# A second MLP whose two layers both run as seven-product block schemes, in alternate phases

## The chip, the cores and the metric

One core of a Trainium2 chip runs the whole program in one launch. The metric is device time in microseconds; the kernel before takes 1431.7 us (median of 3 runs, 1430.7 to 1431.89).

## The reference, cut to what matters

An attention between `x` and a small `state` gives 4352 tokens of 512 values, which go through two MLPs with FF = 2048. The change lies in the second one:

```python
def _moe2_ref(x, w_in, w_out, alpha):        # x 4352 x 512
    h = x @ w_in                             # w_in 512 x 2048
    g = np.maximum(h, 0.0) + alpha * np.minimum(h, 0.0)
    return (g @ w_out).astype(np.float32)    # w_out 2048 x 512
```

## The kernel before, in words

Each matrix product keeps fp32 accuracy by splitting an operand into a high part (`hi_`, an ACT copy that rounds to fp32r) and a low part (`lo_`, a DVE subtraction of two SBUF tiles, raw minus high; in a few places on POOL). Three matmuls replace one: high by high, high by low, low by high.

The first MLP runs in `steps`: nine token tiles times 16 blocks of FF, with the attention, the decoding of weights and the preparation of the second MLP hung onto step numbers by `at(...)`. A tile's result goes to DRAM (`xd`) from `out_end`.

The second MLP is `second()`. Tokens are cut into five superblocks; superblock s has two halves of `HALF[s]` tokens (512, 512, 384, 384, 384). Layer one is a Strassen-Winograd scheme: the two halves of the tokens and the two halves of the contraction make 2 x 2 blocks, and each of the 8 pairs q of FF blocks needs seven products instead of eight. One product is one `h_item`: six matmuls with a weight block standing and `HALF[s]` tokens streaming. `h_after` adds products into the four results and applies the slope (`slope`: ReLU of -h on ACT, then one DVE operation with `beta_sb`). `w_sums` and `w_split` make the weight sums and their high and low parts, again for each of the 40 (s, q). Layer two is direct: `o_item` takes one FF block of one half, its activations standing in 128-token pieces and 512 columns of `w_out` streaming, three matmuls per piece, 16 FF blocks accumulating.

The order is written out by hand. `ev` holds layer one's products at places 0, 1, 2, ... and layer two's items at 36 + 1.75 m, sorted; so both layers alternate item by item, layer two some 36 products behind. Each engine works its own instructions in program order; SP (`ld`) issues nearly all DMAs, in program order too. Tiles come from pools: `U` 80 buffers of 128 x 512, `V` 10 of 128 x 1024, PSUM two pools of four banks (`pa` for accumulators, `pp`). An instruction that needs a buffer waits until its last reader is done.

The lines of the profile: L759 layer one's matmuls, L824 layer two's, L73 the high parts, L76 the low parts, L661 weight sums, L726 sums of x, L768 and L770 the slope, L784 adds from PSUM, L788 a copy from PSUM, L744 and L646 the loads of weights, L847 the stores of the output.

Of the kernel before, what the change touches and what calls it, by code (L numbers as in the profile page):

```python
# [34 lines left out]
ROWS = S + NS  # L35
TOK = NB * ROWS
HALF = [512, 512, 384, 384, 384]
# [3 lines left out]
def kernel_body(ctx: ExitStack, tc: tile.TileContext, x, state, w1i, w1o, w2i, w2o, alpha, out):  # L41
# [55 lines left out]
    wod = dp.tile([NF, 128, 1024], F32, name="wod")  # L97
# [544 lines left out]
    def wr_get(q):  # L642

        for kh in range(2):
            t = U(f"wr{q}{kh}")
            ld.dma_start(out=t, in_=wid[q % 8, kh])  # L646
            WR[q, kh] = t
# [4 lines left out]
    def w_sums(q):  # L652
        r0, r1 = [parts(WR[q, kh]) for kh in range(2)]
        a11, a21, a12, a22 = r0[:, :, 0], r0[:, :, 1], r1[:, :, 0], r1[:, :, 1]
        sa, sb = U(f"sa{q}"), U(f"sb{q}")
        WR[q, 2], WR[q, 3] = sa, sb
        va, vb = parts(sa), parts(sb)
        s2, s1, s3, s4 = va[:, :, 0], va[:, :, 1], vb[:, :, 0], vb[:, :, 1]
        for o, a, b, op in ((s1, a21, a22, ALU.add), (s2, s1, a11, ALU.subtract),
                            (s3, a11, a21, ALU.subtract), (s4, a12, s2, ALU.subtract)):  # L660
            dve.tensor_tensor(out=o, in0=a, in1=b, op=op)  # L661
            yield

    def w_split(q, n):

        t, h = WR.pop((q, n)), U(f"wh{q}{n}", F32R)
        if n == 0:
            t = parts(t)[:, :, 0]
            h, l = [h[:, v * 256:(v + 1) * 256].rearrange("p (k c) -> p k c", k=2) for v in range(2)]
        else:  # L670
            l = U(f"wl{q}{n}", F32R)
        hi_(h, t)
        yield
        yield
        lo_(l, t, h)
        if n == 0:
            WU[q, 0] = h, l
            return
        h, l = parts(h), parts(l)
        for e, k in enumerate({1: (1, 3), 2: (5, 4), 3: (6, 2)}[n]):  # L680
            WU[q, k] = (h[:, :, e], l[:, :, e])

    def pairs(j):
        return 2 * j, 2 * j + 1

    FO = list(range(NF))

    def w2o_put(n):

        raw = G.pop(("dec", ("w2o", FO[n])))  # L690
        h, l = U(f"woh{n}", F32R), U(f"wol{n}", F32R)
        hi_(h, raw)
        WR["o", n] = h, l
        yield
        lo_(l, raw, h)

    def w2o_store(n):
        for e, t in enumerate(WR.pop(("o", n))):
            ld.dma_start(out=wod[FO[n], :, e * 512:(e + 1) * 512], in_=t.bitcast(F32))


    NSUP = len(HALF)

    BASE = [2 * sum(HALF[:s]) for s in (0, 1, 2, 4, 3)]
    C0 = [BASE[s // 2] + (s % 2) * HALF[s // 2] for s in range(2 * NSUP)]
    HO = [0, 5, 4, 6, 1, 2, 3]
    XR, XB, XT, HB, GT, GR, GS, OA = {}, {}, {}, {}, {}, {}, {}, {}
# [4 lines left out]
    def xr_load(s, kh, tk):  # L712
        w = wof(s)
        v = V(f"xr{s}{kh}{tk}")[:, :2 * w].rearrange("p (k c) -> p k c", k=2)
        c0 = C0[2 * s + tk]
        ld.dma_start(out=v, in_=xd[2 * kh:2 * kh + 2, :, c0:c0 + w].rearrange("k p c -> p k c"))
        XR[s, kh, tk] = v

    def x_sums(s, m):

        for kk in range(2):
            b11, b21, b12, b22 = [XR[s, kh, tk][:, kk] for tk in range(2) for kh in range(2)]
            XT[s, m, kk] = U(f"xt{s}{m}{kk}")[:, :wof(s)]
            x, y = {3: lambda: (b22, b12), 2: lambda: (XT[s, 3, kk], b11), 1: lambda: (b12, b11),
                    4: lambda: (b21, XT[s, 2, kk])}[m]()
            dve.tensor_tensor(out=XT[s, m, kk], in0=x, in1=y, op=ALU.add if m == 2 else ALU.subtract)  # L726

    def x_prep(s, step):

        w = wof(s)  # L730
        n = HO[step]
        for kk in range(2):
            b11, b21, b12, b22 = [XR[s, kh, tk][:, kk] for tk in range(2) for kh in range(2)]
            src = {0: b11, 1: b21, 2: b22}.get(n)
            if src is None:
                src = XT[s, {3: 4, 4: 1, 5: 2, 6: 3}[n], kk]
            h, l = U(f"xh{s}{n}{kk}", F32R)[:, :w], U(f"xl{s}{n}{kk}", F32R)[:, :w]
            hi_(h, src)
            lo_(l, src, h, pool if kk else dve)
            XB[s, n, kk] = (h, l)  # L740

    def wo_get(m):
        t = V(f"wv{m}", F32R)
        ld.dma_start(out=t.bitcast(F32), in_=wod[FO[m % NF]])  # L744
        WB["o", m] = t

    def h_item(n):
        q, k = divmod(n, 7)
        s, p = q // 8, HO[k]
        bank = {0: "A", 1: "A", 5: "D", 6: "D", 3: "D", 4: "E", 2: "E"}[p]  # L750
        if p in (0, 5, 4):
            HB[q, bank] = PS(f"hB{q}{p}")
        ps = HB[q, bank][:, :wof(s)]
        wh, wl = WU.pop((q, p))
        m = 0
        for kk in range(2):
            xh, xl = XB[s, p, kk]
            for a, b in ((wh, xh), (wh, xl), (wl, xh)):
                pe.matmul(ps, a[:, kk], b, start=(p in (0, 5, 4) and m == 0), stop=(m == 5),  # L759
                          skip_group_check=True)  # L760
                m += 1

    def slope(q, e, tk, h, g=None):

# [7 lines left out]
    def h_after(n):

        q, k = divmod(n, 7)
        w = wof(q // 8)
        p = HO[k]
        A, D, E = [HB[q, b][:, :w] if (q, b) in HB else None for b in "ADE"]

        def tmp(name):
            GT[q, name] = U(f"{name}_{q}")[:, :w]  # L780
            return GT[q, name]

        def plus(out, a, b):
            dve.tensor_tensor(out=out, in0=a, in1=b, op=ALU.add)  # L784
            return out

        if p == 0:
            act.copy(tmp("p1"), A)  # L788
        elif p == 5:
            plus(tmp("u2"), D, GT[q, "p1"])  # L790
        elif p == 1:
            slope(q, 0, 0, A)
        elif p == 6:
            h = plus(tmp("u3"), D, GT[q, "p1"])
            plus(h, E, h)
            slope(q, 1, 1, h, h)
        elif p == 3:
# [6 lines left out]
    def o_split(m):
        t, f = m // NF, FO[m % NF]
        w = wof(t // 2)
        g = GR.pop((t, f))
        v = V(f"gs{m}", F32R)
        h, l = v[:, :w], v[:, 512:512 + w]
        hi_(h, g)  # L810
        lo_(l, g, h)
        GS[m] = (h, l)

    def o_item(m):
        t, r = divmod(m, NF)
        gh, gl = GS.pop(m)
        wt = WB.pop(("o", m))
        wh, wl = wt[:, :512], wt[:, 512:]
        for k in range(wof(t // 2) // 128):
            if r == 0:  # L820
                OA[k] = pa.tile([128, 512], F32, tag="acc", name=f"accB{t}{k}")
            ks = slice(k * 128, (k + 1) * 128)
            for j, (a, b) in enumerate(((gh[:, ks], wh), (gh[:, ks], wl), (gl[:, ks], wh))):
                pe.matmul(OA[k], a, b, start=(r == 0 and j == 0), stop=(r == NF - 1 and j == 2))  # L824
        if r < NF - 1:
            return
        nk = wof(t // 2) // 128
        for k in range(nk):
            o = U(f"oB{t}{k}")
            last = t == 2 * NSUP - 1 and k == nk - 1  # L830
            if last:
                act.copy(o[:, :256], OA[k][:, :256])
                dve.tensor_copy(o[:, 256:], OA.pop(k)[:, 256:])
            elif k % 2 == 0:
                act.copy(o, OA.pop(k))
            else:
                dve.tensor_copy(o, OA.pop(k))
            b, qq = divmod(C0[t] // 128 + k, 4)
            if b < NB:
                dst = out[b * ROWS:b * ROWS + S, :].rearrange("(p r) c -> p r c", r=4)[:, qq, :]  # L840
            else:
                dst = out.rearrange("(b r) c -> b r c", r=ROWS)[4 * qq:4 * qq + 4, S:, :]
            if last:
                act.dma_start(out=dst[:, :256], in_=o[:, :256])
                ld.dma_start(out=dst[:, 256:], in_=o[:, 256:])
            else:
                ld.dma_start(out=dst, in_=o)  # L847
# [248 lines left out]
```

## Time and profile before

| | |
|---|---|
| median of the runs | 1431.7 us |
| profiled execution, span | 1429.7 us |
| span and what lies around it (the same 2.0 us for the median) | 1431.7 us |
| busy share PE / DVE / ACT / POOL | 98 / 73 / 55 / 6 % |
| second MLP, first to last matmul | 716.3 to 1425.4 us |
| DMA traffic | 253 MB, 177 GB/s in the mean |
| loads of `w_out`'s and `w_in`'s parts in the second MLP | 160 of 512 KB, 80 of 256 KB |

Busy time is the time in which an engine works on at least one instruction. The chain of waits goes back from the last instruction, at each step to what released it. A row of the groups gives line, engine, operation, the tile written and those read, shapes and count, then busy time and the mean of one in ns, then idle time of the engine just ahead of such instructions with what ended it. A row of the timeline gives start, duration, instruction, and how long the engine had been idle. Matmuls overlap, so their price is the distance from start to start.

### The profile page before, as it was taken

The numbers are of one execution on the slowest core, as the hardware profiler recorded it, in microseconds if no ns is written. First come the engines' busy times: TensorE is split into PE (matmuls) and PEld (weight loads), VectorE is DVE, ScalarE is ACT, GpSimd is POOL, SyncE is SP. The second block draws the span as 40 slices with busy tenths as digits, with TensorE's granted clock in tenths as the row PEclk, the third lists the DMA queues.
The fourth block names the chain that finished last, engine by engine and source line by source line (L and its number), as shares of the span: only waits on it lengthen the run. The fifth ranks groups of instructions, "written<-read, shape, count | busy, mean of one in ns | idle before, by whom it ended". The sixth has DMA issues, their size and how long they took to land.

```text
span 1429.7 us, 18991 instructions
## 1 busy us (share of the span) xinstructions
PE 1405.3 (98%) x6548; PEld 1170.0 (82%) x6548; DVE 1044.2 (73%) x1884; ACT 784.4 (55%) x1502; POOL 91.2 (6%) x94
## 2 busy tenths in 40 slices
PE   6799999999999999999999999999999999999998
PEld 4466688888888888888988888888888899989987
DVE  7888685868787888763789786659666976786742
ACT  5566676776776777764644353335433544454431
POOL 1000001121100000000200110002000200010000
PEclk9999999999999999999999999999999999999999
DMA  6898415788744554565323453354545555664545
GB/s 210 309 319 298 119 52 155 212 225 226 216 155 140 162 163 133 163 213 182 120 89 103 155 185 127 125 177 162 177 138 190 201 186 178 201 210 163 184 167 201
DMA packets 146793, 253.43 MB, mean 177 GB/s; under 512 B 47240, under 2 KB 59784, under 8 KB 146696
## 3 DMA queue, kind: packets, MB, share of 16 engines
q1 hardware_dynamic: 107560, 234.54, 49.1%
q0 software_dynamic: 33280, 8.51, 3.2%
q10 hardware_dynamic: 5856, 9.18, 1.7%
q8 instruction: 51, 0.84, 0.3%
q14 instruction: 46, 0.38, 0.1%
HBM read 195.96 MB, written 55.57 MB: 176 GB/s over the span
## 4 chain that ended last, share of the span: by engine, by line
PE 89%; DVE 6%; DMA 2%; ACT 1%; issue 1%; ACTq 0%; SPq 0%; DVEq 0%
PE accB L824 24%; PE accA L613 21%; PE hB L759 21%; PE hA L84 13%; PE accA L605 3%; PE vgp L84 1%; PE sr L84 1%; PE sc L84 1%; DMA vr<-vd 1%; DVE xt L726 1%; DVE gs L76 1%; DMA vd<-vgo 1%; DVE xl L76 1%; PE et L198 0%; DMA wr_wi<-in_moe_w_in_dram 0%
## 5 line engine op out<-in xcount | busy, mean ns | idle before, releaser
L824 PE MATMUL accB<-wv,gs 128*128 128x512 f32 x1632 | 397.2, 391 | 0.0
L824 PEld LDWEIGHTS accB<-wv,gs 128*128 128x128 f32 x1632 | 305.1, 188 | 59.3
L759 PE MATMUL hB<-xh,wh 128*128 128x384 f32 (+1 forms) x640 | 216.9, 359 | 1.0 <-DVE u L784 0.9
L759 PE MATMUL hB<-xl,wh 128*128 128x384 f32 (+1 forms) x560 | 200.2, 357 | 0.0
L759 PE MATMUL hB<-xh,wl 128*128 128x384 f32 (+1 forms) x480 | 170.9, 358 | 0.0
L581 DVE SCALAR_TENSOR_TENSOR g<-y,hA 128x512 f32<-128x512 f32 (+1 forms) x144 | 94.0, 653 | 65.3 <-ACT y L579 64.9
L759 PEld LDWEIGHTS hB<-xh,wh 128*128 128x128 f32 x640 | 119.5, 188 | 17.4 <-DVE u L784 3.3
L578 ACT ACTIVATE y<-hA 128x512 f32<-128x512 f32 (+1 forms) x144 | 82.5, 573 | 87.4 <-PE hA L84 86.1
L768 ACT ACTIVATE m<-u 128x384 f32<-128x384 f32 (+1 forms) x80 | 45.4, 568 | 134.5 <-DVE u L784 134.4
L76 DVE TENSOR_TENSOR gl<-g,gh 128x512 fp32r<-128x512 f32 (+1 forms) x128 | 93.0, 726 | 31.6 <-ACT gh L73 29.7
L759 PEld LDWEIGHTS hB<-xl,wh 128*128 128x128 f32 x560 | 105.1, 188 | 12.6
L76 DVE TENSOR_TENSOR gs<-u,gs 128x384 fp32r<-128x384 f32 (+1 forms) x80 | 48.6, 609 | 72.5 <-ACT gs L73 72.1
L759 PEld LDWEIGHTS hB<-xh,wl 128*128 128x128 f32 x480 | 90.0, 188 | 7.6
L73 ACT CAST gh<-g 128x512 fp32r<-128x512 f32 (+1 forms) x128 | 75.6, 591 | 28.6 <-DVE g L581 26.8
L579 ACT ACTIVATE y<-y 128x512 f32<-128x512 f32 (+1 forms) x144 | 87.6, 608 | 4.3
L73 ACT CAST gs<-u 128x384 fp32r<-128x384 f32 (+1 forms) x80 | 44.4, 556 | 82.0 <-PE accB L824 80.9
L784 DVE TENSOR_TENSOR u<-hB,p 128x384 f32<-128x384 f32 (+1 forms) x80 | 48.5, 607 | 40.9 <-PE hB L759 40.8
L770 DVE SCALAR_TENSOR_TENSOR u<-m,beta_sb,u 128x384 f32<-128x384 f32 (+1 forms) x80 | 56.0, 700 | 25.1 <-ACT m L768 24.2
L605 PE MATMUL accA<-g,wf_w1o 128*128 128x512 f32 x128 | 60.7, 607 | 4.6 <-DVE wf_w1o L398 4.6
L493 ACT COPY vgo<-vgp 128x512 f32<-128x512 f32 x64 | 37.2, 585 | 43.0 <-PE vgp L84 21.9
L76 POOL TENSOR_TENSOR xl<-xr,xh 128x384 fp32r<-128x384 f32 (+1 forms) x15 | 18.4, 1225 | 621.4 <-ACT xh L73 621.4
L73 ACT CAST wh<-sa 128x512 fp32r<-128x512 f32 x40 | 24.8, 621 | 56.7 <-DVE sa L661 51.1
(960 smaller groups left out, 3063.5 us busy)
## 6 DMA issues: line engine op xcount, KB each, us to landing
wv<-wod SPq DMA_DIRECT2D x160, 512.0 KB
wr<-wid SPq DMA_DIRECT2D x80, 256.0 KB
vd<-vgo SPq DMA_DIRECT2D x64, 256.0 KB
x<-in_x_dram SPq DMA_DIRECT2D x30, 512.0 KB
vr<-vd SPq DMA_DIRECT2D x56, 256.0 KB
out_dram<-oB SPq DMA_DIRECT2D x33, 256.0 KB
wr_wi<-in_moe_w_in_dram SPq DMA_DIRECT2D x16, 512.0 KB
wr_w1o<-in_moe_w_out_dram SPq DMA_DIRECT2D x16, 512.0 KB
```

Source lines behind the costliest of these rows:

```text
L73: act.copy(h, raw)
L76: (eng or dve).tensor_tensor(out=l, in0=raw, in1=h.bitcast(F32), op=ALU.subtract)
L84: pe.matmul(ps, a, b, start=(k == 0), stop=(k == n - 1))
L578: act.activation(out=y[:, :n], in_=ps, func=AF.Relu, bias=0.5, scale=0.5)
L579: act.activation(out=y[:, :n], in_=y[:, :n], func=AF.Square)
L581: dve.scalar_tensor_tensor(out=g[:, :n], in0=y[:, :n], scalar=1.0, in1=ps, op0=ALU.min, op1=ALU.max)
L605: pe.matmul(ACC[k], w[:, k * 128:(k + 1) * 128], g, start=(f == 0), stop=(f == NF - 1))
L613: pe.matmul(ACC[k][:, :n], a, b, start=(f == 0 and j == 0), stop=(f == NF - 1 and j == 2))
L759: pe.matmul(ps, a[:, kk], b, start=(p in (0, 5, 4) and m == 0), stop=(m == 5), skip_group_check=True)
L770: dve.scalar_tensor_tensor(out=g, in0=m, scalar=beta_sb[:, f:f + 1], in1=h, op0=ALU.mult, op1=ALU.add)
L784: dve.tensor_tensor(out=out, in0=a, in1=b, op=ALU.add)
L824: pe.matmul(OA[k], a, b, start=(r == 0 and j == 0), stop=(r == NF - 1 and j == 2))
```

## The change

Layer two becomes the same kind of scheme, with `w_out` standing: for each of 8 pairs k of FF blocks seven products, each product two column halves j, three matmuls each, `HALF[s]` tokens streaming (now 448, 448, 448, 416, 416). Product i accumulates over the 8 pairs in PSUM, then `o_after` adds it to the others; the result is in columns by tokens, so `out_put` transposes it in 32 x 32 blocks on DVE and stores it from SP in DMAs of 32 partitions, in runs of 32 values (128 bytes). `out_store(1)` issues one such store per event, ahead of the event's weight loads.

The phases alternate: all 56 layer-one items of a superblock (order `LS`), then its 56 layer-two items; only (7,3) and (7,2) of layer one come between layer two's first five items. The splits of layer two's first three items are issued after the epilogue of (7,6), later ones three items ahead.

The activations' sums (`g_comb`, two SBUF inputs, in place) run on POOL: one per pair in layer one's phase, and one in each of the first 24 items of layer two. The next superblock's x is summed on DVE, twice as wide, and split (half of the low parts on POOL) from item 10 of layer two on, every fourth item.

Weight sums are made once, on POOL: those of `w_in` in the first superblock, with high and low parts stored to `w1d` and loaded again by the other superblocks (256 KB per product), those of `w_out` during the first MLP, stored to `w2d`. Loads run six events ahead. `out_end` writes its tiles in natural token order.

```diff
-HALF = [512, 512, 384, 384, 384]
+HALF = [448, 448, 448, 416, 416]
...
-                act.copy(o[:, :n], ACC.pop(k)[:, :n])
+            if t < NB:
+                act.copy(o.rearrange("q (p r) -> q r p", r=4), ACC.pop(k).rearrange("q (r p) -> q r p", r=4))
...
+    def four_sums(key, a11, a12, a21, a22, view):
...
+            pool.tensor_tensor(out=o, in0=a, in1=b, op=op)
+    def put(src, name, view, dst):
+        t = U(name, F32R)
+        h, l = t[:, :256], t[:, 256:]
+        hi_(view(h), src)
+        yield
+        lo_(view(l), src, view(h))
+        ld.dma_start(out=dst, in_=t.bitcast(F32))
+        return t
...
+    PO = [0, 1, 5, 6, 4, 3, 2]
+    SLOT = [(0, 0), (1, 0), (3, -1), (5, 0), (2, -1), (4, 0), (6, 0)]
+    LS = [(q + d, p) for q in range(9) for p, d in SLOT if 0 <= q + d < 8]
...
+    def h_after(s, q, p):
...
+        elif p == 6:
+            act.copy(tmp("u3"), A)
+            h = plus("c22", E, GT.pop((q, "u3")))
+            slope(s, q, 1, 1, h, h)
+        elif p == 3:
+            slope(s, q, 1, 0, A)
+        elif p == 2:
+            h = plus("c12", E, GT.pop((q, "u2")))
+            slope(s, q, 0, 1, h, h)
+            g_comb(q, 3)
+    def g_comb(q, m):
+        b11, b21, b12, b22 = [GR[q, e, tk] for tk in range(2) for e in range(2)]
+        x, y, op = {3: (b22, b12, ALU.subtract), 2: (b12, b11, ALU.add),
+                    4: (b21, b11, ALU.subtract), 1: (b22, b11, ALU.subtract)}[m]
+        pool.tensor_tensor(out={3: b12, 2: b11, 4: b21, 1: b11}[m], in0=x, in1=y, op=op)
+    def o_split(s, i, k):
...
+        hi_(h, src)
+        lo_(l, src, h)
+    def o_item(s, i, k):
...
+        for j in range(2):
...
+            for n, (a, b) in enumerate(((wh, gh), (wh, gl), (wl, gh))):
+                pe.matmul(ps, a[:, js], b, start=(p != 2 and k == 0 and n == 0), stop=(k == 7 and n == 2),
+        if k == 7:
+            for j in range(2):
+                o_after(s, p, j)
...
+    def out_put(s, oh, j, tk, c):
+        t = U(f"ot{s}{oh}{j}{tk}")[:, :w]
+        dve.transpose(out=t, in_=c)
...
+            for a in range(4):
+                src = t[32 * a:32 * a + 32, c0 - first:c0 - first + n].rearrange("p (b j) -> p b j", j=32)
+                OS.append((dst[4 * g + a], src))
...
     def second():
+        ahead = 6
+        for s in range(NSUP):
+            os = [("o", s, i, k) for i in range(7) for k in range(8)]
+            hs = [("h", s, q, p) for q, p in LS]
+            ev += hs[:-2]
+            ev += [os[0], os[1], hs[-2], os[2], os[3], hs[-1]] + os[4:]
...
+        for n, (kind, s, a, b) in enumerate(ev):
+            out_store(1)
+            while nl < len(loads) and nl <= at_load.get(ev[min(n + ahead, len(ev) - 1)], -1):
+                (w2_get if loads[nl][0] == "o" else w1_get)(*loads[nl][1:])
+                nl += 1
+            if kind == "h":
+                h_item(s, a, b)
+                h_after(s, a, b)
...
+                if (a, b) == (7, 6):
+                    o_split(s, 0, 0)
+                    o_split(s, 0, 1)
+                    o_split(s, 0, 2)
             else:
+                m = 8 * a + b
+                if m + 3 < 56:
+                    o_split(s, *divmod(m + 3, 8))
+                if a in (0, 1, 2):
+                    g_comb(b, (2, 4, 1)[a])
+                o_item(s, a, b)
+                if s + 1 < NSUP and m >= 10 and (m - 10) % 4 == 0 and (m - 10) // 4 < len(XSTEPS):
+                    fn, arg = XSTEPS[(m - 10) // 4]
+                    fn(s + 1, arg)
+        out_store(len(OS))
```

## Rows read from the trace of the kernel before

**Rows 1.** The page: busy time, share of the span, instructions of each engine.
```profile
PE 1405.3 (98%) x6548; PEld 1170.0 (82%) x6548; DVE 1044.2 (73%) x1884; ACT 784.4 (55%) x1502; POOL 91.2 (6%) x94
```
**Rows 2.** The page: chain of waits, shares of the span by line.
```profile
PE accB L824 24%; PE accA L613 21%; PE hB L759 21%; PE hA L84 13%; PE accA L605 3%; PE vgp L84 1%; PE sr L84 1%; PE sc L84 1%; DMA vr<-vd 1%; DVE xt L726 1%; DVE gs L76 1%; DMA vd<-vgo 1%; DVE xl L76 1%; PE et L198 0%; DMA wr_wi<-in_moe_w_in_dram 0%
```
**Rows 3.** Stretches: length, busy PE, PEld, DVE, ACT, POOL, clock, DMA share, GB/s.
```profile
720.40:1425.40 705.00, 703.98 (x3309) 607.81 (x3307) 499.47 (x908) 301.11 (x592) 37.01 (x28) 1.00 0.49 166
800.00:900.00 100.00, 99.86 (x440) 82.36 (x440) 75.67 (x121) 45.61 (x83) 10.26 (x7) 1.00 0.44 154
```
**Rows 4.** Waits of PE's weight loads, 720 to 1430: total, times, longest.
```profile
PEld hB L759 <- DVE u L784: 3.3, 7, 0.6
```
**Rows 5.** Timeline of PE, where layers of 512 and of 384 tokens run.
```profile
902.09 2.88 PE L824 MATMUL accB<-wv,gs 128*128 128x512 f32 x12
904.81 0.39 PE L759 MATMUL hB<-xh,wh 128*128 128x512 f32 x1
...
1000.54 0.33 PE L759 MATMUL hB<-xh,wh 128*128 128x384 f32 x1
...
1002.65 2.92 PE L824 MATMUL accB<-wv,gs 128*128 128x512 f32 x12
```
**Rows 6.** Groups by shape: operations that the change adds, moves or removes.
```profile
L788 ACT COPY p<-hB 128x384 f32<-128x384 f32 x24 | 11.5, 480 | 9.7 <-PE hB L759 9.4
L784 DVE TENSOR_TENSOR u<-hB,p 128x384 f32<-128x384 f32 x48 | 26.6, 554 | 21.8 <-PE hB L759 21.8
L768 ACT ACTIVATE m<-u 128x384 f32<-128x384 f32 x48 | 25.2, 525 | 73.5 <-DVE u L784 73.5
L770 DVE SCALAR_TENSOR_TENSOR u<-m,beta_sb,u 128x384 f32<-128x384 f32 x48 | 31.0, 646 | 13.1 <-ACT m L768 12.6
L76 DVE TENSOR_TENSOR gs<-u,gs 128x384 fp32r<-128x384 f32 x48 | 26.5, 555 | 41.3 <-ACT gs L73 41.3
L76 DVE TENSOR_TENSOR gs<-u,gs 128x512 fp32r<-128x512 f32 x32 | 22.1, 690 | 31.1 <-ACT gs L73 30.8
L76 DVE TENSOR_TENSOR wh<-wr,wh 128x256 fp32r<-128x256 f32 x40 | 16.6, 416 | 0.1
L255 DVE STREAM_TRANSPOSE at<-st 128x512 f32<-128x512 f32 x14 | 9.8, 703 | 0.0
```
**Rows 7.** Stretches around the clock's fall: columns as in rows 3.
```profile
40.70:45.40 4.70, 0.12 (x2) 0.08 (x1) 4.57 (x10) 0.62 (x1) 0.00 (x0) 1.00 0.63 180
45.40:49.00 3.60, 3.60 (x6) 1.41 (x7) 1.21 (x4) 1.74 (x3) 0.00 (x0) 0.53 0.94 288
```
**Rows 8.** Timelines of DVE and POOL where both work at once.
```profile
1118.06 1.84 DVE L726 TENSOR_TENSOR xt<-xt,xr 128x384 f32<-128x384 f32 x2
1118.04 1.44 POOL L76 TENSOR_TENSOR xl<-xr,xh 128x384 fp32r<-128x384 f32 x1 [121.89 <-ACT xh L73]
...
1253.35 0.54 DVE L784 TENSOR_TENSOR u<-hB,p 128x384 f32<-128x384 f32 x1
1252.12 2.17 POOL L76 TENSOR_TENSOR xl<-xt,xh 128x384 fp32r<-128x384 f32 x1 [3.20 <-ACT xh L73]
```
**Rows 9.** Timeline of POOL: operations that met no DVE operation of that kind.
```profile
830.06 1.29 POOL L76 TENSOR_TENSOR xl<-xr,xh 128x512 fp32r<-128x512 f32 x1 [0.82 <-ACT xh L73]
...
991.04 1.01 POOL L76 TENSOR_TENSOR xl<-xr,xh 128x384 fp32r<-128x384 f32 x1 [0.36 <-ACT xh L73]
```
**Rows 10.** The stretch of the first MLP that makes layer two's weights.
```profile
460.00:660.00 200.00, 200.00 (x914) 166.51 (x913) 157.23 (x278) 139.95 (x255) 2.34 (x2) 1.00 0.52 167
```
**Rows 11.** The page's DMA queues: packets, MB, share of 16 engines.
```profile
q1 hardware_dynamic: 107560, 234.54, 49.1%
q0 software_dynamic: 33280, 8.51, 3.2%
```
**Rows 12.** Timeline of the end.
```profile
1425.45 0.37 ACT L832 COPY oB<-accB 128x256 f32<-128x256 f32 x1 [0.77 <-PE accB L824]
1426.31 0.33 SPq L845 DMA_DIRECT2D out_dram<-oB  x1
```

More of the change, by code (lines that the diff above doesn't have):

```diff
@@ L645, in wr_get @@
             t = U(f"wr{q}{kh}")
-            ld.dma_start(out=t, in_=wid[q % 8, kh])
+            ld.dma_start(out=t, in_=wid[q, kh])
             WR[q, kh] = t
@@ L650, in parts, with halves @@
         return t.rearrange("p (k e c) -> p k e c", k=2, e=2)
[L652 to L658, printed above, removed]
+    def halves(t):
+        return [t[:, h * 256:(h + 1) * 256].rearrange("p (k c) -> p k c", k=2) for h in range(2)]
@@ L659, in w_sums @@
+    def four_sums(key, a11, a12, a21, a22, view):
+        sa, sb = U(f"sa{key}"), U(f"sb{key}")
+        s1, s2, s3, s4 = [view(t[:, h * 256:(h + 1) * 256]) for t in (sa, sb) for h in range(2)]
         for o, a, b, op in ((s1, a21, a22, ALU.add), (s2, s1, a11, ALU.subtract),
                             (s3, a11, a21, ALU.subtract), (s4, a12, s2, ALU.subtract)):
-            dve.tensor_tensor(out=o, in0=a, in1=b, op=op)
-            yield
[L664 to L681, printed above, removed]
@@ new lines, in four_sums, with w1_sums @@
+        return {0: a11, 1: a12, 2: s4, 3: a22, 4: s1, 5: s2, 6: s3}
+    def put(src, name, view, dst):
[6 more added lines that the diff above has]
+        return t
+    def w1_sums(q):
+        r0, r1 = [parts(WR.pop((q, kh))) for kh in range(2)]
+        WS[q] = four_sums(f"a{q}", r0[:, :, 0], r1[:, :, 0], r0[:, :, 1], r1[:, :, 1],
+                          lambda t: t.rearrange("p (k c) -> p k c", k=2))
@@ new lines, in w1_put, with w2_sums, w2_put @@
+    def w1_put(q, *ps):
+        for p in ps:
+            t = yield from put(WS[q].pop(p), f"wu{q}{p}", lambda t: t.rearrange("p (k c) -> p k c", k=2), w1d[q, p])
+            WU[0, q, p] = t
+            yield
+    def w2_sums(q):
+        r0, r1 = [G.pop(("dec", ("w2o", 2 * q + e))) for e in range(2)]
+        WS["o", q] = four_sums(f"o{q}", r0[:, :256], r1[:, :256], r0[:, 256:], r1[:, 256:], lambda t: t)
+    def w2_put(q, *ps):
+        for p in ps:
+            yield from put(WS["o", q].pop(p), f"wo{q}{p}", lambda t: t, w2d[q, p])
+            yield
@@ L713, in xr_load @@
         w = wof(s)
-        v = V(f"xr{s}{kh}{tk}")[:, :2 * w].rearrange("p (k c) -> p k c", k=2)
-        c0 = C0[2 * s + tk]
-        ld.dma_start(out=v, in_=xd[2 * kh:2 * kh + 2, :, c0:c0 + w].rearrange("k p c -> p k c"))
+        v = V(f"xr{s}{kh}{tk}")[:, :2 * w]
+        c0 = BASE[s] + tk * w
+        ld.dma_start(out=v.rearrange("p (k c) -> p k c", k=2),
+                     in_=xd[2 * kh:2 * kh + 2, :, c0:c0 + w].rearrange("k p c -> p k c"))
         XR[s, kh, tk] = v
-    def x_sums(s, m):
-        for kk in range(2):
[L722 to L752, printed above, removed]
+    def x_comb(s, m):
+        b11, b21, b12, b22 = [XR[s, kh, tk] for tk in range(2) for kh in range(2)]
+        x, y, op = {3: (b22, b12, ALU.subtract), 2: (b12, b11, ALU.add),
+                    4: (b21, b11, ALU.subtract), 1: (b22, b11, ALU.subtract)}[m]
+        dve.tensor_tensor(out={3: b12, 2: b11, 4: b21, 1: b11}[m], in0=x, in1=y, op=op)
@@ new lines, in w1_get, with w2_get, h_item @@
+    def w1_get(s, q, p):
+        t = U(f"wu{s}{q}{p}", F32R)
+        ld.dma_start(out=t.bitcast(F32), in_=w1d[q, p])
+        WU[s, q, p] = t
+    def w2_get(s, i, k):
+        t = U(f"wv{s}{i}{k}", F32R)
+        ld.dma_start(out=t.bitcast(F32), in_=w2d[k, PO[i]])
+        WB[s, i, k] = t
+    def h_item(s, q, p):
+        bank = {0: "A", 5: "A", 6: "A", 3: "A", 1: "B", 4: "E", 2: "E"}[p]
+        new = p in (0, 1, 4)
+        if new:
+            HB[q, bank] = acc_ps(f"hB{s}{q}{p}") if p == 1 else PS(f"hB{s}{q}{p}")
@@ L772, in h_after @@
[L772 to L785, printed above, removed]
+                pe.matmul(ps, a[:, kk], b, start=(new and m == 0), stop=(m == 5), skip_group_check=True)
@@ new lines, in h_item, with slope, tmp, plus @@
+                m += 1
+    def slope(s, q, e, tk, h, g=None):
+        f = 2 * q + e
+        m = U(f"m{s}{q}{e}{tk}")[:, :wof(s)]
+        act.activation(out=m, in_=h, func=AF.Relu, scale=-1.0)
+        g = GR[q, e, tk] = m if g is None else g
+        dve.scalar_tensor_tensor(out=g, in0=m, scalar=beta_sb[:, f:f + 1], in1=h, op0=ALU.mult, op1=ALU.add)
+    def h_after(s, q, p):
+        w = wof(s)
+        A, B, E = [HB[q, b][:, :w] if (q, b) in HB else None for b in "ABE"]
+        def tmp(name):
+            GT[q, name] = U(f"{name}{s}_{q}")[:, :w]
+            return GT[q, name]
+        def plus(name, a, b):
+            o = tmp(name)
+            dve.tensor_tensor(out=o, in0=a, in1=b, op=ALU.add)
+            return o
+        if p == 0:
+            act.copy(tmp("p0"), A)
+        elif p == 1:
+            h = plus("c11", B, GT.pop((q, "p0")))
+            slope(s, q, 0, 0, h, h)
+        elif p == 5:
+            act.copy(tmp("u2"), A)
+        elif p == 6:
[8 more added lines that the diff above has]
+            g_comb(q, 3)
@@ L787, in h_after, with o_after, plus @@
+    def o_after(s, p, j):
+        w = wof(s)
+        ps = OA["E" if p in (2, 4) else p, j][:, :w]
+        def plus(name, b):
+            o = OC[name, j] = U(f"{name}{s}{j}")[:, :w]
+            dve.tensor_tensor(out=o, in0=ps, in1=b, op=ALU.add)
+            return o
         if p == 0:
-            act.copy(tmp("p1"), A)
+            o = OC["p0", j] = U(f"op0{s}{j}")[:, :w]
+            act.copy(o, ps)
+        elif p == 1:
+            out_put(s, 0, j, 0, plus("c11", OC["p0", j]))
         elif p == 5:
-            plus(tmp("u2"), D, GT[q, "p1"])
-        elif p == 1:
-            slope(q, 0, 0, A)
+            plus("u2", OC.pop(("p0", j)))
@@ L804, in o_split @@
[L804 to L835, printed above, removed]
-            else:
[L837 to L840, printed above, removed]
-            else:
[L842 to L847, printed above, removed]
@@ L986, in kernel_body @@
             at(gi(8, 4 * blk - 9 + c), w1s_load, blk, c)
-    w2 = [("w2i", n // 2, n % 2) for n in range(16)] + [("w2o", f) for f in FO]
+    w2 = [("w2i", n // 2, n % 2) for n in range(16)] + [("w2o", f) for f in range(NF)]
     for n, key in enumerate(w2):
```

173 lines of the change are left out of this document (84 added, 89 removed).

## The prediction, before the change was run

> **What bounds the kernel now.** I read the page's shares first: PE 98% busy, DVE 73%, ACT 55%, POOL 6% [rows 1]. A busy PE need not be the limit, so the chain of waits came second: nearly all of its lines are PE's, and the second MLP alone (L824 and L759) holds 45% [rows 2]. The stretches say the same of the part that changes: in the 705 us from 720.4 to 1425.4 PE idles 1 us at full granted clock, DVE works 499, ACT 301, POOL 37, DMA runs at 0.49 [rows 3]. The longest wait of PE's queue there is 3.3 us in all, on DVE and not on a DMA [rows 4]. So the second MLP costs what its matmuls cost, and everything else hides. A matmul's price is read from start to start in the timeline: twelve 512-wide ones in 2.72 us (227 ns), twelve 384-wide ones in 1000.54 to 1002.65, 2.11 us (176 ns) [rows 5]. The straight line between gives 201 ns at 448 columns and 188.5 at 416.
>
> **The change, part by part.** *Second layer in seven products.* Before, from 720.4 on: 1632 matmuls of 227 ns in L824 and 1680 in L759, 705 us in all, 707 with the few that ran earlier. After: each layer has 56 items of six matmuls in each superblock, 336 x (3 x 0.201 + 2 x 0.1885) = 329.5 us, both 659. **PE: -47.8 us.** This part is sure; the question is whether PE stays fed.
>
> *Phases.* Before, layers were interleaved, so that a slow chain in one was covered by matmuls of the other. Now the first product of layer two follows layer one's last item (7,6) at once, and its operands stand behind that item's epilogue in ACT's and DVE's order: copy of bank A (0.48 at 384 columns), add (0.55), ReLU (0.53), slope (0.65), then the low part (0.555); the high part fits in beside the slope. The low part takes 0.135 more at 512 [rows 6], so 0.07 more for each at 448: 0.55 + 0.62 + 0.60 + 0.72 + 0.62 = 3.1 us of empty PE (hand-overs, and the one matmul that needs only the high part, about cancel), five times: **+15.5 us**. Nothing covers it: the two items held back for that place, (7,3) and (7,2), come behind the first and the third pair. The clock may add to it: it fell to 0.53 for 3.6 us after 4.7 us almost without work [rows 7], and 3.6 us at 0.53 cost 1.7. 3.1 us is shorter than that pause, so I count nothing and keep 5 x 1.7 = 8.5 us for the upper end.
>
> *Splits and combinations.* Layer two now needs 56 splits per superblock (32 before), and 32 sums of the activations, which go to POOL: one per pair in layer one's phase, 24 in the first 24 items of layer two's. By busy time DVE gets lighter, because 40 rounds of weight sums and splits shrink to eight: each round's low parts alone (3 x 0.69 + 0.42 [rows 6]) come to 2.5 us, 100 in all. But rows show something that shares hide: a DVE operation with both inputs in SBUF and a POOL operation exclude each other. At 1118.0 POOL starts while DVE's first of two sums runs; POOL takes 1.44 instead of 1.01 us, DVE's pair 1.84 instead of 1.02. An operation that reads PSUM runs through (L784 at 1253.35) [rows 8]. POOL alone needs 1.01 at 384 and 1.29 at 512 [rows 9], so 1.15 at 448 and 1.08 at 416. The low part in the split is such a DVE operation; behind a POOL operation it streams 0.41 us at 384 (1119.48 to 1119.89), so some 0.48 at 448.
>
> POOL's sum for an item waits only for that item's low part, so both engines want the port item after item. Alternating, one item costs 1.15 + 0.48 = 1.63 us where PE needs 6 x 0.201 = 1.21. In one superblock this lasts from item 7 to item 31: 21 sums and 3 low parts of x on POOL (24 x 1.15 = 27.6), 27 low parts (13.0) and two double-wide sums of x (1.9) on DVE: 42.5 us against 24 x 1.21 = 29.0. The lead at item 7 is small, since its split stands behind the epilogue of (7,2): three items, 3.6 us, less 0.62 + 0.60 + 0.72 + 0.62, about 1 us. So 12.5 late. If only the lengthening of a single collision counts (0.82 at 384, so 0.96 at 448, on the 0.54 that a low part takes from start to start) it is 24 x 0.96 + 27 x 0.54 + 2.0 = 39.6, 9.5 late. I take 11.5 for the three superblocks of 448, 10.5 for the fourth, and 6 for the last, which prepares no x: **+51 us**. The bounds are 0 (a collision gives nothing back) and 57 (12.5 and its like throughout). The remaining 24 items carry no sums: DVE needs some 26 us there and PE 29, so PE is the limit again, and what it lost isn't won back.
>
> Behind this stands a rule of the Trainium skill (SBUF — State Buffer, section "Who interferes with whom"): whoever of DVE and GpSimd issues first holds the shared port for its whole instruction, and the other blocks fully. By it the two alternate, and the sum has the 51. One row differs: at 1252.12 POOL needs 2.17 us instead of 1.01 [rows 8], so it let 1.16 us of DVE work go first, two operations more than the one in hand; by that row DVE keeps the port and POOL drains later, and the term is about 22.
>
> *Weights made once.* In the first superblock each pair has 7 high and 7 low parts of 256 columns (0.41 and 0.42) and 4 sums on POOL; DVE and POOL together want the port about 8 of a pair's 8.4 us, so +2. The other set is made in the first MLP, 460 to 660, where DVE is busy 157 of 200 us [rows 10]: instead of 16 x 0.69 it gets 56 x 0.42 (+12.5), and POOL holds the port for 32 sums of 0.73 (line through 1.01 and 1.29), 23 us. That fits into the 43 idle, in the mean; PE's lead there is one step, so +2 with bounds 0 and 6. The strided copies of oA have two matmul groups of cover: 0.
>
> *Loads and stores.* Loads grow from 160 of 512 KB and 80 of 256 KB to 504 of 256 KB, 105 to 132 MB: the part's 117 MB (705 us at 166 GB/s) become 144 in some 700 us, 0.6 of the DMA engines by the 0.49 [rows 3]. The output leaves as 69,632 pieces of 128 B. No row has such pieces alone; per packet the queues show between 0.032 x 16 x 1429.7 us / 33,280 = 22 ns and 0.491 x 16 x 1429.7 / 107,560 = 104 ns [rows 11], that is 96 or 453 us of all engines. I take the nearer, 22 (mean 256 B): together 0.75, which hides; the far end is the third rival. The transposes (0.70 [rows 6]) are 40 in 330 us, inside the 26 us above.
>
> *Tail.* Now 1425.45 to 1429.7 lie behind the last matmuls [rows 12]. After: add, transpose, add, transpose (2 x 0.62 + 2 x 0.63) and then the last four of eight stores, at 0.33 to 0.5 us each, 4.1 us to the last issue's end, against 1.2 (1425.45 to 1426.64): **+3 us**.
>
> **The sum** is made for the profiled execution, span 1429.7, which lies 2.0 under the median of 1431.7; the same 2.0 is carried over. 1431.7 - 47.8 + 15.5 + 51 + 4 + 3 = **1457 us**.
>
> **Rivals.** *First: DVE keeps the port.* As at 1252.12, POOL gets in only when DVE pauses. Over a whole phase of layer two the port is then wanted 31 x 1.15 + 63 x 0.48 + 4 x 0.95 = 70 us against 67.5 of PE; by item 29, when the last kind of sum falls due, 21 x 1.15 + 33 x 0.48 + 1.9 = 42 against 35 and the lead: about 5.5 us late in four superblocks. 1431.7 - 47.8 + 15.5 + 22 + 7 = 1428. For it: that row. Against: 1118.04, where POOL got in ahead of the second of two DVE operations [rows 8].
>
> *Second, faster: the collisions hit DVE, not PE.* In 800 to 900 seven POOL operations ran among DVE's, and PE lost 0.14 us [rows 3]. If DVE's lead over PE swallows them here too, the term is 0: 1431.7 - 47.8 + 15.5 + 7 = 1406. It decides if PE idles under 0.1 us per item in the first 24 items. Against: seven operations there in 100 us, 24 in 29 here, and POOL alone wants 27.6 of these.
>
> *Third: late weights.* Each store waits on SP for its transposes, and the loads for six events ahead (7.2 us) stand behind it in the same queue. If a product's end, four a superblock, costs PE one item: 20 x 1.2 = 24 us, 1481. It decides from where a load lands later than six items less that wait. For it: two issues per item in one queue, small pieces. Against: no wait of PE on a DMA now. The Trainium skill (DMA: Bandwidth & Descriptors, "Specifications") asks for 512 B per transfer, below which a read-modify-write comes in; no run here shows its price, and by it this rival would be likelier than I put it.
>
> **How the numbers follow.** Forecast 0.48, own range 1443 to 1472 (the port term from 41 to 57, the weights' 4 from 0, the clock's 8.5). First rival 0.17, second 0.20, third 0.15. The range from 1404 to 1481 leaves out some half of the second (under 1404) and half of the third (over 1481). Within 0.2% of before (2.9 us, about what a measurement of this kernel can tell from none) only the first rival can come, 0.05; below it are the second and part of the first, 0.27; slower 0.68.
>
> **What would show it.** Layer matmuls at 201 and 188.5 ns when dense, 3360 of them. A gap of some 3 us on PE at each of five changes from layer one to layer two, ended by the split's DVE operation. In the first half of each phase of layer two, PE waiting on the split, DVE's low parts at 1.3 to 1.6 us instead of 0.62, and POOL near 90% busy; in the second half neither. PE's waits on weight loads near nothing. I am wrong if PE runs dense through those first 24 items with POOL and DVE overlapping, or if DMA ends PE's waits.

## The result: 1.4% slower

The changed kernel takes 1452.1 us (median of 4 runs, 1450.3 to 1455.2), the one before 1431.2 beside it: a ratio of 1.0142, 95% interval 1.0126 to 1.0158. The forecast was 1457. The profiled execution took 1451.2 us, its span is 1449.4.

The page of the changed kernel, its shares by engine; they answer to [rows 1]:
```profile
PE 1390.5 (96%) x6596; PEld 1197.4 (83%) x6596; DVE 1082.6 (75%) x1765; ACT 841.7 (58%) x1628; POOL 352.9 (24%) x318
```
PE works 15 us less, the span is 20 us longer. The second MLP is where this happens. Stretches, columns as in [rows 3]: the whole second MLP, then, in the second superblock's phase of layer two, the items with sums and the items without.
```profile
723.20:1441.60 718.40, 686.74 (x3362) 635.34 (x3360) 527.05 (x750) 336.65 (x676) 263.83 (x212) 0.98 0.72 227
...
951.30:983.00 31.70, 27.45 (x120) 24.60 (x119) 28.76 (x28) 13.87 (x26) 27.31 (x20) 0.89 0.18 50
990.00:1022.00 32.00, 32.00 (x156) 29.07 (x155) 23.93 (x38) 16.31 (x32) 6.05 (x5) 1.00 0.77 235
```
Before, PE idled 1 us there [rows 3]; now 32. Where sums run, DVE and POOL are busy 91% and 86% and PE idles 4 us of 32; where none run, PE idles nothing. The DMA share of the first of the two stretches, 0.18, is a surprise: the loads stop.

What PE waited for in the second MLP (total us, times, longest), where [rows 4] had nothing above 0.6:
```profile
PE accB L830 <- DMA wv<-w2d: 13.7, 5, 3.6
PE accB L830 <- DVE gs L76: 7.4, 4, 1.9
PE hB L757 <- ACT u L788: 4.5, 3, 1.8
PE hB L757 <- ACT p L783: 1.7, 5, 1.1
```
The longest entry is a DMA, five times: once in each superblock, in front of item 22 of layer two. And what SP, which issues both loads and stores, waited for:
```profile
SPq L887 <- DVE ot L867: 170.5, 11, 28.3
```
In each superblock SP stands for 23 to 28 us before the first store (L887), until DVE has transposed that tile (L867). Every load behind that store stands with it. In the third superblock, timeline of SP and then the wait of PE in it:
```profile
1122.72 0.83 SPq L887 DMA_DIRECT2D out_dram<-ot  x2
1123.65 0.88 SPq L743 DMA_DIRECT2D wv<-w2d  x2
1124.58 0.42 SPq L887 DMA_DIRECT2D out_dram<-ot  x1
1125.10 0.39 SPq L743 DMA_DIRECT2D wv<-w2d  x1
```
```profile
PE accB L830 <- DMA wv<-w2d: 3.1, 1, 3.1
```
Why the transpose is late is seen on DVE and POOL. First DVE, then POOL, near item 16 of the first superblock:
```profile
813.09 1.57 DVE L76 TENSOR_TENSOR xl<-xr,xh 128x448 fp32r<-128x448 f32 x1
814.59 1.57 DVE L76 TENSOR_TENSOR gs<-m,gs 128x448 fp32r<-128x448 f32 x1
818.32 2.03 DVE L720 TENSOR_TENSOR xr<-xr,xr 128x896 f32<-128x896 f32 x1 [2.16 <-POOL xl L76]
```
```profile
812.65 4.53 POOL L805 TENSOR_TENSOR m<-m,c 128x448 f32<-128x448 f32 x3
817.14 1.14 POOL L76 TENSOR_TENSOR xl<-xr,xh 128x448 fp32r<-128x448 f32 x1
818.25 1.14 POOL L805 TENSOR_TENSOR m<-m,c 128x448 f32<-128x448 f32 x1
```
A low part takes 1.57 us beside a sum, as forecast (1.3 to 1.6), and three sums take 4.53. The sum of x waits 2.16 us for a POOL operation queued behind the sums (an ordinary wait on its result), then collides as well (2.03 us; 1.08 in the mean once the sums are gone). PE's gap at 818.7 to 820.9 is the end of this.

The clock followed the gaps. Two of seven stretches at the lower level (1.2 GHz) between 720 and 1441, columns as in [rows 3]:
```profile
979.30:982.70 3.40, 3.33 (x9) 3.04 (x10) 3.40 (x4) 0.57 (x1) 2.28 (x2) 0.50 0.99 259
1126.10:1129.50 3.40, 2.93 (x8) 2.66 (x9) 3.40 (x4) 0.31 (x1) 2.81 (x2) 0.50 0.95 274
```
Six of the seven last 3.4 us and one 6.8, and each begins in, or up to 1.4 us behind, a gap on PE that is 2 to 4 us long from start to start. Before, the granted clock was full throughout this part.

Adding up the distances between PE's starts, 3359 of them at their dense 202.7 and 188.3 ns make 661.5 us, and from the first start to the last the second MLP took 718.1. The other 56.6 are 34.5 in gaps (each over 0.3 us), 11.7 in matmuls at half clock and 10.4 in smaller delays.

### The profile page after: what moved, and what is told of

Read it like the earlier page. It is cut to its first block, busy times and chain, and to the rows that moved or that the text cites. A ratio compares the mean times of both kernels' runs of the same rounds, so it can differ in the third digit from the quotient of the medians.

```text
span 1449.4 us, 20876 instructions
## 1 busy us (share of the span) xinstructions
PE 1390.5 (96%) x6596; PEld 1197.4 (83%) x6596; DVE 1082.6 (75%) x1765; ACT 841.7 (58%) x1628; POOL 352.9 (24%) x318
## 5 line engine op out<-in xcount | busy, mean ns | idle before, releaser
L830 PE MATMUL accB<-gs,wv 128*128 128x448 f32 (+1 forms) x1680 | 347.8, 368 | 21.2 <-DMA wv<-w2d 13.7
L830 PEld LDWEIGHTS accB<-gs,wv 128*128 128x128 f32 x1680 | 322.2, 193 | 44.4 <-issue 14.3
L757 PE MATMUL hB<-xh,wu 128*128 128x448 f32 (+1 forms) x1120 | 323.5, 364 | 10.4 <-ACT u L788 4.5
L757 PEld LDWEIGHTS hB<-xh,wu 128*128 128x128 f32 x1120 | 210.7, 189 | 33.4 <-ACT u L788 6.3
L805 POOL TENSOR_TENSOR c<-c,c 128x448 f32<-128x448 f32 (+1 forms) x120 | 157.0, 1323 | 276.0 <-DVE c L766 188.0
L757 PE MATMUL hB<-xl,wu 128*128 128x448 f32 (+1 forms) x560 | 201.8, 360 | 0.0
L76 DVE TENSOR_TENSOR gs<-c,gs 128x448 fp32r<-128x448 f32 (+1 forms) x200 | 164.4, 851 | 29.3 <-ACT gs L73 28.2
L73 ACT CAST gs<-c 128x448 fp32r<-128x448 f32 (+1 forms) x200 | 109.7, 556 | 126.5 <-PE accB L830 99.2
L766 DVE SCALAR_TENSOR_TENSOR c<-m,beta_sb,c 128x448 f32<-128x448 f32 (+1 forms) x120 | 90.5, 754 | 60.6 <-ACT m L764 60.0
L579 ACT ACTIVATE y<-hA 128x512 f32<-128x512 f32 (+1 forms) x144 | 82.5, 573 | 71.8 <-PE hA L84 71.7
L757 PEld LDWEIGHTS hB<-xl,wu 128*128 128x128 f32 x560 | 105.6, 189 | 5.0
L76 DVE TENSOR_TENSOR gs<-m,gs 128x448 fp32r<-128x448 f32 (+1 forms) x80 | 72.2, 920 | 12.6 <-ACT gs L73 11.6
```

The costliest lines, as they stand in the source:

```text
L73: act.copy(h, raw)
L76: (eng or dve).tensor_tensor(out=l, in0=raw, in1=h.bitcast(F32), op=ALU.subtract)
L579: act.activation(out=y[:, :n], in_=ps, func=AF.Relu, bias=0.5, scale=0.5)
L757: pe.matmul(ps, a[:, kk], b, start=(new and m == 0), stop=(m == 5), skip_group_check=True)
L805: pool.tensor_tensor(out={3: b12, 2: b11, 4: b21, 1: b11}[m], in0=x, in1=y, op=op)
L830: pe.matmul(ps, a[:, js], b, start=(p != 2 and k == 0 and n == 0), stop=(k == 7 and n == 2), skip_group_check=True)
```

## The experiments

All were timed beside the kernel before; ratios are to it, with the 95% interval in brackets, and times are medians.

**e1, stores behind later loads.** The stores of a product are held in their list until item 32, then go out two per item, each fixed behind the load issued last.
```diff
-            out_store(1)
+            if kind == "h" or not 16 <= 8 * a + b < 32:
+                out_store(1 + (kind == "o"))
...
-            ld.dma_start(out=dst, in_=src)
+            with tc.issue_after(LOAD[0].ins):
+                ld.dma_start(out=dst, in_=src)
```


> The output's stores of a superblock's first product end are issued on SP behind the weight loads of layer two's items up to 38 instead of 22; two go out per item then. Theory A (late weights): in the changed kernel SP stands 23 to 28 us before the first of these stores in each superblock, and PE then waits for the weights of item 22 (five gaps of 1.9 to 3.8 us, 14.5 us together, and five stretches at half clock behind them, some 7 us): these five gaps go and the time falls from 1452 by 14 to 21 us, to 1431-1438. Rival B (the port term): DVE is late by as much at that place, and behind the loads PE waits for the split instead: the time stays within 5 us of 1452.

Measured: 1.0404 (1.0389 to 1.0420), 1490.3 us. Neither theory had it slower. Waits of PE in it, second MLP:
```profile
PE accB L831 <- DMA wv<-w2d: 21.7, 17, 3.9
PE accB L831 <- DVE gs L76: 13.9, 12, 1.9
PE hB L758 <- DMA wu<-w1d: 11.7, 11, 2.2
```
And SP's timeline in the second superblock, once it moves again:
```profile
1016.34 0.80 SPq L889 DMA_DIRECT2D out_dram<-ot  x2
1017.24 0.38 SPq L744 DMA_DIRECT2D wv<-w2d  x1
1017.67 0.91 SPq L889 DMA_DIRECT2D out_dram<-ot  x2
1018.68 0.39 SPq L744 DMA_DIRECT2D wv<-w2d  x1
1019.11 0.92 SPq L889 DMA_DIRECT2D out_dram<-ot  x2
```
The five gaps before item 22 are gone, but SP stands 21.4 us at the next product's store instead (a later wait, the same kind), and then two stores and a load cost it 1.44 us (1017.67 to 1019.11) where PE takes 1.22 for an item. Of the 33 us of waits for weights 14 come straight behind that stand (four of 3.1 to 3.9 us); the other 19 come where SP works off the backlog of loads at that rate. The edit changed two things at once, place and rate, so it says nothing on A against B; that is left to e5. It does show that SP has little to spare: one store and one load take 0.96 of 1.22 us, so loads that fell behind catch up slowly.

**e2, the sums on DVE.** One word in `g_comb`.
```diff
-        pool.tensor_tensor(out={3: b12, 2: b11, 4: b21, 1: b11}[m], in0=x, in1=y, op=op)
+        dve.tensor_tensor(out={3: b12, 2: b11, 4: b21, 1: b11}[m], in0=x, in1=y, op=op)
```


> The 32 sums of activations per superblock run on DVE instead of POOL; nothing else is changed. Theory B (port term): low parts fall back from 0.85 us in the mean to 0.62, the gaps at item 17 of layer two and at products 35 to 38 of layer one shrink (8 and 9 us together, and their clock), and the transposes for the first store come earlier, so the waits for weights shrink too: 1425 to 1440. Rival A (late weights, whatever the port does): only the gaps that no load ends go, at most 10 us: 1442 or more. Rival C (DVE is full): 32 x 0.62 = 20 us more of DVE work per superblock costs more than the collisions did: slower than 1452.

Measured: 0.9827 (0.9809 to 0.9844), 1406.4 us, 46 us under the changed kernel and 25 under the one before. The low part in the split, in groups by shape, first in the changed kernel, then in e2; and e2's stretch of the second MLP:
```profile
L76 DVE TENSOR_TENSOR gs<-c,gs 128x448 fp32r<-128x448 f32 x120 | 101.0, 871 | 11.5 <-ACT gs L73 10.9
```
```profile
L76 DVE TENSOR_TENSOR gs<-c,gs 128x448 fp32r<-128x448 f32 x120 | 74.7, 642 | 7.3 <-ACT gs L73 6.8
L805 DVE TENSOR_TENSOR c<-c,c 128x448 f32<-128x448 f32 x72 | 44.7, 628 | 0.5
```
```profile
720.00:1396.00 676.00, 669.66 (x3390) 631.65 (x3388) 531.09 (x919) 338.06 (x681) 57.09 (x52) 1.00 0.77 242
```
DVE carries 160 more operations and is busy as long as before them (from 720 us to the end 531.7 us against 530.7 in the changed kernel): what it took on it had been spending on collisions. PE's waits for weights fall from 13.7 to 2.1 us, the clock stays full to the last matmul. It came out better than B said because B counted only the gaps that no load ended, plus a share.

**e3, x's low parts on DVE too** (`lo_(l, r, h)` in `x_split`).

> As the run before, and the low parts of x's second halves run on DVE too, so that POOL does nothing in the second MLP but the weight sums of its first superblock. If DVE's waits for POOL's low part of x (2.2 us ahead of the sum of x at 818.3) carry the gap at item 17, that gap goes wholly and the time is 2 to 6 us under the run with the sums alone on DVE. If DVE is by then the bound (7 x 0.54 = 3.8 us more per superblock), it is not under it.

Measured: 0.9815 (0.9791 to 0.9839), 1404.7 us; the interval overlaps that of e2. In e2 the gap that the expectation puts at item 17 (at 818.7 in the changed kernel, in front of the second matmul of item 16 counted from 0) had already gone; POOL's 28 low parts of x, four or more items apart, cost nothing that can be measured.

**e4, the splits where the source has them.**
```diff
+            with tc.issue_after(END[s]["act"].ins):
+                hi_(h, src)
+            with tc.issue_after(END[s]["dve"].ins):
+                lo_(l, src, h)
```
(for the first eight items; `END[s]` are the ReLU and slope of (7,6)).

> The splits of layer two's first eight items keep the place that the source gives them, behind the ReLU and the slope of layer one's item (7,6); in the changed kernel as built they stand some 20 products earlier. Theory D (my step of the phase change was right but for the order): a gap of about 3 us appears at each of the five changes of phase, 15.5 us, less the gaps at products 35 to 38 of layer one that the early splits cause (9 us, and some clock): 1455 to 1467. Rival (other work covers the change in any order): no gap above 1 us there, and the time is 1452 or less.

Measured: 1.0295 (1.0277 to 1.0312), 1474.4 us: slower than both theories said, and the gap is not where D had it. Timeline of PE at the first change of phase, then of DVE:
```profile
792.19 0.36 PE L758 MATMUL hB<-xh,wu 128*128 128x448 f32 x1
793.18 0.47 PE L758 MATMUL hB<-xh,wu 128*128 128x448 f32 x1 [0.62 <-ACT u L791]
```
```profile
794.42 0.68 DVE L767 SCALAR_TENSOR_TENSOR c<-m,beta_sb,c 128x448 f32<-128x448 f32 x1 [0.64 <-ACT m L765]
795.03 2.65 DVE L76 TENSOR_TENSOR gs<-c,gs 128x448 fp32r<-128x448 f32 x3
```
PE loses 0.78 us at each change, in front of one of the two held-back items: as built, all but two matmuls of (7,3) and (7,2) run before layer two's first item, and the two items cover 2.4 us of the chain. The rest of the 22 us comes later:
```profile
PE accB L837 <- DVE gs L76: 23.1, 16, 4.7
PE accB L837 <- DMA wv<-w2d: 14.2, 6, 8.3
```
Waits for splits grow from 7.4 to 23.1 us. Timeline of PE in the second superblock's phase of layer two, first in the changed kernel, then in e4:
```profile
952.68 7.66 PE L830 MATMUL accB<-gs,wv 128*128 128x448 f32 x37
```
```profile
952.80 7.16 PE L837 MATMUL accB<-gs,wv 128*128 128x448 f32 x29
```
In the changed kernel items 4 to 15 take 1.22 us each, which is dense; in e4 items 5 to 14 take 1.48 to 1.51 with two exceptions (1.76 and 2.09), each behind its split. So the early splits and sums gave DVE and POOL a lead, and that lead was hiding part of the port term.

**e5, stores that never wait.** The stores read a tile that is ready (`stT`), each fixed behind the load six items ahead; their sizes and number stay.
```diff
-                src = t[32 * a:32 * a + 32, c0 - first:c0 - first + n]
+                src = stT["t"][32 * a:32 * a + 32, 512 + c0 - first:512 + c0 - first + n]
```


> The changed kernel with its sums on POOL, but the stores read a tile that was ready long before (512 columns of the turned state) instead of the turned products, each held on SP right behind the load six items ahead; so the output's values are left out, its transfers and the transposes are not. The sums' port term was 46 us by the run with the sums on DVE; the question is by which way it reaches PE. Theory A: about half of it comes through SP, which stands up to 28 us before a store whose transpose DVE makes late, so that the weights behind it are late: PE's waits for weights (13.7 us) and the half clock behind them (7 us) go, and the time is 1427 to 1438. Rival B: DVE's lateness alone decides, and PE waits for splits instead: 1445 to 1453.

Measured: 0.9995 (0.9986 to 1.0005), 1431.6 us, 20.5 under the changed kernel. Waits of PE:
```profile
PE accB L831 <- DVE gs L76: 10.8, 10, 2.1
PE hB L758 <- ACT u L789: 4.4, 3, 1.8
```
No wait for a weight is left, one stretch at half clock remains of seven, and the second MLP takes 701.2 us from its first matmul to its last instead of 718.1. That is 17 us through SP (theory A). Another 5 are the tail, which here ends 2.8 us behind the last matmul instead of 7.8, since the last stores wait for nothing: they belong to the edit. From 701.2 down to e2's 671.1 the other 30 us of the port's 47 (12.6 in layer one's phases, 17.5 in layer two's) reach PE through late splits and PSUM banks that ACT and DVE free late, as far as the list of waits tells.

**e6, sums that nobody reads.**
```diff
+        o = U(f"sc{i}{q}")[:, :x.shape[-1]]
+        pool.tensor_tensor(out=o, in0=x, in1=GS[i, q][1].bitcast(F32), op=op)
```


> The 24 sums per superblock of layer two's phase stay on POOL, each starts behind the low part of the same item as now, but writes a tile that nobody reads, and takes that low part as its second input; layer two so works on activations that are not combined. POOL's load on the port is unchanged, and no instruction of DVE, ACT or PE waits for one of these sums. Theory P (the shared port): low parts still take 0.8 us or more in the mean, and the time stays within 1438 to 1455. Rival W (DVE and PE wait for POOL's results, which come late because POOL is slow): with the waits gone the time falls to that of the sums on DVE, 1400 to 1412.

Measured: 1.0137 (1.0120 to 1.0154), 1451.6 us: the same as the changed kernel. DVE's low part and POOL's sum in it:
```profile
L76 DVE TENSOR_TENSOR gs<-c,gs 128x448 fp32r<-128x448 f32 x120 | 104.8, 909 | 9.5 <-ACT gs L73 8.6
```
```profile
L810 POOL TENSOR_TENSOR sc<-c,gs 128x448 f32<-128x448 f32 x48 | 70.5, 1498 | 0.0
```
P's forecast holds: where nobody reads these sums nothing is won. But the run is not as clean as the expectation has it. A sum reads the low part's tile, of which there are ten, so ACT waits for POOL before it writes a later high part there; and six or seven of the sums per superblock that the changed kernel runs in layer one's phase start only in layer two's here, so that layer one's phases lose 6.9 us on PE instead of 20.8 and layer two's 47.8 instead of 35.8. That the times agree so closely is partly chance. ACT's and DVE's waits in e6, then in the changed kernel:
```profile
ACT gs L73 <- POOL sc L810: 92.1, 83, 3.2
DVE gs L76 <- ACT gs L73: 37.9, 78, 2.7
```
```profile
ACT gs L73 <- POOL c L805: 3.0, 1, 3.0
DVE gs L76 <- ACT gs L73: 39.8, 78, 3.2
```
Little of ACT's waiting reaches DVE, which waits for high parts no longer than in the changed kernel. What speaks more plainly against W is the changed kernel itself: there ACT waits 4.3 us in all for POOL's sums, and DVE and PE never do (DVE waits 11.6 us for POOL's low parts of x).

**e7, only sparse sums on POOL.**
```diff
+        eng = pool if m == 3 else dve
```


> Only the 24 sums per superblock of layer two's phase go to DVE; the 8 of layer one's phase, one per pair and some 8 us apart, stay on POOL. If the port costs only where both engines want it item after item, this is as fast as with all sums on DVE: 1403 to 1410. If every collision costs PE its 0.96 us, 40 of them cost up to 36 us: 1420 to 1442.

Measured: 0.9863 (0.9844 to 0.9882), 1413.5 us, 7 over e2: neither forecast. Forty sums eight microseconds apart cost about 0.18 us each if all of it is put down to them, not nothing and not 0.96. In this kernel DVE does wait for POOL's result, which later sums on DVE read; groups of DVE:
```profile
L806 DVE TENSOR_TENSOR c<-c,c 128x416 f32<-128x416 f32 x32 | 19.2, 604 | 8.5 <-POOL c L806 8.2
```
How much of the 7 us is that wait and how much collisions isn't told apart.

## Why the prediction was right, and where it was wrong

*The matmuls (-47.8): about right, -44.1.* Dense they cost 202.7 and 188.3 ns (12 in 2.43 us from 1091.51 to 1093.94), where the straight line gave 201 and 188.5; and the few that ran ahead of 720.4 were four, 0.9 us, so that the part before took 706.0 us and not 707.

*The port (+51): right in its cause, and near in size (46 us by e2 against the changed kernel), but largely by other ways than the sum has.* On PE alone the five superblocks lost 10.3, 12.6, 9.4, 7.3 and 7.6 us to it, 47.0 in all (11.5 three times, 10.5 and 6 forecast). The first half of each phase of layer two loses, the second doesn't, as said; but not item by item. Of the 47.0 us 30 fell on items 16 to 23 and under 2 on items 0 to 15, which run all but dense beside DVE and POOL (one of my two signs of being wrong, met for 16 of the 24 items), and 14 fell in layer one's phases, where the sum has none; PE's waits for splits were 7.4 us in all. What the sum had wrong was the lead of about 1 us at item 7, worked out from the split standing behind an epilogue: with six or more splits and some six of the 24 sums of each superblock made before layer two begins the lead was larger, and the collisions fell on DVE alone until item 16. Without that lead (e4) the items do go at POOL's pace, as worked out. The alternation is cheaper than worked out: five sums and the low parts between them took 7.38 us on POOL, 1.48 each, not 1.63:
```profile
1063.24 7.38 POOL L805 TENSOR_TENSOR c<-c,c 128x448 f32<-128x448 f32 x5 [7.39 <-PE hB L757]
```
That would be 0.27 per item over PE's 1.21, some 6.5 us in the 24 items of one superblock. Much of the 46 came by ways that the prediction didn't tie to the port: late transposes hold SP's stores, the stores hold the weights (17 us by e5), and the gaps lower the clock (11.7 us of PE time, all gone in e2, for which I had kept 8.5 only at the upper end). The rule of the Trainium skill (SBUF — State Buffer, "Who interferes with whom") that one engine blocks the other for its whole instruction agrees with these rows to about 0.15 us: 1.15 for a sum alone and 0.48 of streaming would make 1.63, against 1.48.

*The changes of phase (+15.5): wrong, 0.* The failed step is "its operands stand behind that item's epilogue in ACT's and DVE's order". They don't. I had taken the order from the source; the built program has the first splits and some sums some 20 products earlier, where what they read is ready. Timeline of DVE there, and of PE and ACT at the change itself:
```profile
1063.03 3.61 DVE L76 TENSOR_TENSOR gs<-c,gs 128x448 fp32r<-128x448 f32 x3
```
```profile
1091.31 0.36 PE L757 MATMUL hB<-xh,wu 128*128 128x448 f32 x1
1091.51 2.59 PE L830 MATMUL accB<-gs,wv 128*128 128x448 f32 x12
1093.94 0.37 PE L757 MATMUL hB<-xh,wu 128*128 128x448 f32 x1
```
```profile
1091.71 0.53 ACT L790 COPY u<-hB 128x448 f32<-128x448 f32 x1 [1.20 <-PE hB L757]
```
Layer two starts before ACT has copied the last of layer one. Even in the source's order the gap at the change would have been 0.78 five times (e4), since the two held-back items move as well; the other 18 of e4's 22 us come behind it, at splits and weights. What I wrote ahead of the prediction, that the order is the one written out by hand, is true of the intent and not of the program.

*Loads and stores (hidden; the third rival at 24): wrong apart from the port, right beside it.* DMA ends PE's longest waits, by which I had said I would be wrong. But that rival had a cost at every product's end whatever DVE did. In e2 SP still stands up to 22 us before a store, and PE waits 2.1 us for weights in all. The stand is harmless while DVE transposes in time: six loads ahead cover it. It was a path of the port term, not a term of its own. Of the rule on pieces under 512 B (DMA: Bandwidth & Descriptors, "Specifications", in the Trainium skill) no run shows the price apart; in e5 the same 128-byte pieces leave beside the loads, and PE waits for no weight.

*Weights (+4) and tail (+3): about right.* Where the first MLP makes layer two's weights, the stretch that answers to [rows 10] is
```profile
460.00:660.00 200.00, 199.68 (x908) 164.94 (x907) 168.16 (x313) 150.53 (x288) 32.99 (x35) 1.00 0.55 184
```
DVE is up 10.9 us (12.5 forecast), POOL 31 (23), PE idles 0.3. The first MLP's own matmuls end 3.7 us later (723.2 against 719.5, without the four of the second MLP among them), and 1.5 of that is there at its first product, before anything that changed; so it takes 2.2 us more. In the other runs, where it is the same, it ends between 721.8 and 726.3, so that 2 us is no more than what varies. With the sums off POOL (e2) the first superblock's layer one takes 71.7 us against 68.9 in the third: together 5.0 instead of 4. The tail is 7.8 us behind the last matmul instead of 4.3, +3.5; it is twelve stores in SP's timeline, which answers to [rows 12]:
```profile
1440.81 5.95 SPq L887 DMA_DIRECT2D out_dram<-ot  x12
```

*The sum.* The spans differ by 19.7, which is within 0.1 -44.1 (matmuls), +47.0 (port), +9.5 (what PE still loses in e2, its weights included), +2.2 (first MLP), +3.5 (tail), +1.5 (the start, ahead of anything that changed). So 15.5 us that never came were in part made up by 4 on the matmuls, 7.5 of scattered waits, 1.5 at the start and under 1 on first MLP and tail, less 4 on the port. The nearness of 1457 to 1452 is in part luck, and so is that of 47 to 51.

*The first rival* (DVE keeps the port, 1428) fell: the engines alternate. *The second* (collisions hit DVE, not PE, 1406) has the time of e2, the kernel without those collisions; with them PE idled 4.3 us over the 20 items of the stretch above (120 matmuls), 0.21 each against its limit of 0.1, and so it fell too. It was right for items 4 to 15, though, and 2.3 of those 4.3 us are the wait for a weight, which no rival tied to the port.

## What to carry to other kernels

Count how often two engines want the same port per item of the bottleneck engine, not their shares: at one sum per 1.2 us item POOL's 24% of busy time cost 46 us, and moving the same work to the busier engine won all of it back. When a queue carries both loads and stores that wait for computed data, a delay on the computing engine turns into late loads; check the issue rate too (here 0.39 and 0.43 us of 1.22). And before pricing a hand-over from the source's order, look at the order in the program as built.

## What the runs showed that was not expected

- DVE's busy time rose by 1 us when 160 operations of about 0.63 us were added (e2): in the changed kernel a quarter of what it showed in the splits was waiting for the port. Busy time of DVE doesn't tell work from blocked work.
- Stretches at 1.2 GHz began after gaps on PE of 2 to 4 us in the middle of otherwise dense work (seven in the changed kernel's second MLP, none in that of e2 and e3); four gaps of 2.0 to 2.3 us (at 829.5, 1112.2, 1214.4 and 1253.8) were not followed by one.
- A store costs SP 0.42 to 0.43 us to issue whether it holds 4 KB or 56, about as long as a load of 256 KB (0.39 us).
